# Query transposes of the first two batches by DMA, with weights and loads reordered around them

## The chip, the cores and the metric

The kernel runs on one core of a Trainium2 chip. A core has five engines with instruction queues of their own: PE (TensorE, matmuls), DVE (VectorE), ACT (ScalarE), POOL (GpSimd) and SP (SyncE), which here only issues DMAs. An engine runs its instructions in the order in which they were written; one that waits for data holds up all behind it. Transfers between memory and the core run on 16 DMA engines that POOL's, SP's and ACT's queues share. [...]

The metric is the device time in microseconds of one execution; lower is better.

## The reference

A linear attention with position-dependent features feeds a feed-forward network without a nonlinearity between its last two weights:

```python
def phi(x, c, s):
    r = np.maximum(x, 0.0)
    return np.concatenate([r * c, r * s], axis=-1)   # c, s: cos and sin by position
q_p = phi(q, cos_w, sin_w)
k_p = phi(k, cos_w, sin_w)
kv = np.einsum('bhsf,bhsd->bhfd', k_p, v)
z = np.sum(k_p, axis=2)
num = np.einsum('bhsf,bhfd->bhsd', q_p, kv)
den = np.einsum('bhsf,bhf->bhs', q_p, z)[..., None] + 1e-06
x = (num / den), heads side by side: (4608, 512)
a = x @ w1
b = x @ w2
h = a * b @ w3
return (h @ w_out).astype(np.float32)
```

There are 8 batches of 576 positions, 8 heads of 64, and weights of 512 x 1024 (w1, w2), 1024 x 1024 (w3) and 1024 x 512 (w_out). Inputs and output are float32.

## The kernel before

**Tiling.** A batch's 576 positions are cut into five chunks: four of 128 and one half chunk of 64 (chunk 4). Odd batches begin with the half chunk. The 4608 tokens are nine token tiles of 512. Token tile 0 holds batch 0's chunks 0 to 3; tile 1 holds batch 0's half chunk in its columns 0 to 63, then batch 1's half chunk and its chunks 0, 1 and 2; batch 1's chunk 3 opens tile 2.

**A batch's attention.** POOL issues its loads (`load`), two DMAs for each of k, q and v: the first brings 320 positions to partitions 0 to 63, the second 256 positions to partitions 64 to 127. The DMAs convert to bf16. `prep_k` and `prep_q` make a chunk's features, the cosine half on DVE, the sine half on ACT (L263, L267). `prep_v` copies v beside a column of ones (L287), on DVE for batches 0 and 1, on POOL later. `kv_chunk` multiplies keys by values on PE (L295), and both ACT and DVE copy the sum out. The query features must be transposed to put features on partitions: either on PE with a copy out of PSUM (`q_tr`, L326, L328, L329), or by a DMA transpose that SP issues (L281). `num` (L355) multiplies them by the key-value sum on PE, and DVE divides by the denominator (L371 to L373). `x_tr` transposes the result into the token tile `xT`, again on PE (L407, copy L409) or by a DMA transpose from SP (L403).

Which way a transpose goes depends on the batch. Queries: all five chunks of batch 0 and the first three of batch 1 go through PE, the last two of batch 1 and everything later by DMA (`dma_q`). x: batch 0 and batch 1 but for its chunk 3 go through PE, the rest by DMA.

**The feed-forward network.** For each token tile, `ffn_groups` is a generator: 64 matmuls of x with w1 and w2 (L452), products on ACT and DVE (L457, L458, L505, L509), then 32 matmuls with w34 = w3 @ w_out (L522). w34 is made once, within token tile 0: eight blocks of w3 are transposed on PE (`w3_tr`, L218, copied out by DVE) and multiplied by w_out (`w34_mm`, L230, copied out by ACT at L233). w34_mm of a block has two parts: part 0 uses the first four row groups of w_out, part 1 the last four.

**The order of work.** Nothing is scheduled automatically. `ffn_groups` yields after each group of matmuls, and after yield number s the program writes whatever stands in `slots[s]`. Token tile 0 has slots 0 to 39: w34 is made in slots 16 to 31 (two per block), the last matmuls of the tile stand in slots 32 to 39. Tile 1 begins with slot 40; each later tile has 24 slots. `at(s, ...)` puts a call into a slot; `plan` does so for a batch: kf, qf and vc are the slots of key features, query features and value copies, kv of the key-value matmuls, nu of `num`, xt of `x_tr`. A slot sets only the place in each engine's queue: an instruction runs when its engine reaches it and its data is there. SP's queue holds nothing but two early loads, the transposes and the last stores.

**Loads.** POOL's loads wait on one of eight semaphores in rotation, so a load is issued only once the one eight places before it has landed. `other_loads` issues the rest of w1, w2, then w3 and w_out, with batch 1's keys in between. Loads of batch 2 and later are held back: `plan_loads` puts a one-element copy on ACT (`mark`, L555) into a slot, and POOL waits for that copy (L557) before it issues the load. Stores of the output are held back in the same way until late.

Of the kernel before, what the change touches and what calls it, by code (L numbers as in the profile page):

```python
# [23 lines left out]
def columns_of(b, c):  # L24


    if b % 2 == 0:
        return 128 * c
    return 0 if c == 4 else 64 + 128 * c
# [39 lines left out]
def kernel(  # L69
# [41 lines left out]
    def load(b, which, part=None):  # L111
        for name in which:
            src = {"k": k, "v": v, "q": q}[name]
            if part != 1:
                raw[b, name] = ld.tile([P, H, NCH, D], BF16, name=name + "s",
                                       bufs=2 if name == "q" else 1)
                nc.gpsimd.dma_start(
                    out=raw[b, name][0:64, :, :, :].rearrange("p h j d -> p h (j d)"),
                    in_=src[b, :, 0:320, :].rearrange("h (p j) d -> p h (j d)", j=5))
            if part != 0:  # L120
                nc.gpsimd.dma_start(
                    out=raw[b, name][64:128, :, 0:4, :].rearrange("p h j d -> p h (j d)"),
                    in_=src[b, :, 320:S, :].rearrange("h (p j) d -> p h (j d)", j=4))
# [17 lines left out]
    def load_w3(jp, n):  # L141
        nc.gpsimd.dma_start(out=w3b[:, jp:jp + n, :],
                            in_=moe_w3[ds(jp * P, n * P), :].rearrange("(b p) l -> p b l", p=P))

    def load_wout():
        nc.gpsimd.dma_start(out=woutb[:], in_=moe_w_out.rearrange("(c p) m -> p c m", p=P))

    k0 = raw[0, "k"] = wst.tile([P, H, NCH, D], FP32, name="kf")
    q0 = raw[0, "q"] = ld.tile([P, H, NCH, D], BF16, name="qs", bufs=2)
# [47 lines left out]
    def other_loads(behind):  # L197

        seen = sm.tile([P, 1], BF16, name="seen", bufs=1)
        nc.gpsimd.tensor_copy(out=seen[:], in_=behind)  # L200
        nc.gpsimd.dma_start(out=w2b[:, :, ds(512, 256)], in_=w2v[:, :, ds(512, 256)])  # L201
        load_w12(768, 256)
        for jp in range(2):
            load_w3(jp, 1)
        load_wout()
        for jp in range(2, 4):
            load_w3(jp, 1)
        load(1, "k")
        for jp in range(4, 8, 2):
            load_w3(jp, 2)  # L210


    w3Ts = {}
# [22 lines left out]
    def order_of(b):  # L236

        return [0, 1, 2, 3, 4] if b % 2 == 0 else [4, 0, 1, 2, 3]

    def dma_q(b):  # L240

        return order_of(b)[5 if b < 1 else 3 if b == 1 else 0:]

    feat = {}

# [7 lines left out]
    def att_of(b):  # L253
        if b not in att:
            att[b] = {"qpT": phi.tile([P, H, S], BF16, name="qpT"), "x": {}}
        return att[b]

    def features(b, dst, src, c, cos=True, sin=True, scalar_heads=H):
# [6 lines left out]
        if sin:  # L265
# [3 lines left out]
            if n < H:  # L269
                nc.vector.tensor_scalar(out=dst[:R, c, n:H, D:F], in0=src[:R, n:H, c, :],  # L270
                                        scalar1=0.0, scalar2=sinv[:R, at:at + 1],
                                        op0=ALU.max, op1=ALU.mult)

    def prep_k(b, c):
        features(b, feat_of(b)[0], raw[b, "k"], c)

    def prep_q(b, c):
        features(b, feat_of(b)[1], raw[b, "q"], c)
        if c in dma_q(b):
            R = ROWS[c]  # L280
            nc.sync.dma_start_transpose(out=att_of(b)["qpT"][:, :, ds(columns_of(b, c), R)],  # L281
                                        in_=feat[b][1][:R, c].rearrange("p h f -> p (h f)"))

    def prep_v(b, c):
        R = ROWS[c]
# [35 lines left out]
    def q_tr(b, c, evac=True):  # L321
        R = ROWS[c]
        qp = feat[b][1]
        pst = ps_tr.tile([P, 8, 128], BF16, name="pst")
        for h in range(H):
            nc.tensor.transpose(pst[:, h, :], qp[:, c, h, :], identb[:])  # L326
        dst, src = att_of(b)["qpT"][:, :, ds(columns_of(b, c), R)], pst[:, :, 0:R]
        on_vector = lambda: nc.vector.tensor_copy(out=dst, in_=src)  # L328
        on_scalar = lambda: nc.scalar.copy(out=dst, in_=src)  # L329
        if evac:  # L330
            on_vector()
        return on_vector, on_scalar
# [10 lines left out]
    def num(b, c, chain=True, in_two=False):  # L343
        rows = out_rows(b, c)
        R = ROWS[c]
        at = columns_of(b, c) - rows.start
        qpT, kvs = att[b]["qpT"], att[b]["kvs"]
        if b == 0 and c == 0:
            nt = ps_first.tile([P, 2, 512], FP32, name="pfirst")
        else:  # L350
            pool = more_att[0] if more_att and order_of(b).index(c) % 2 == 0 else ps_att
            nt = None if in_two else pool.tile([P, 2, 512], FP32, name="pnum")
        banks = [ffn_tile(), ffn_tile()] if in_two else [nt[:, g, :] for g in range(2)]
        for h in range(H):
            nc.tensor.matmul(banks[h // 4][:, ds((h % 4) * 65, 65)], lhsT=qpT[:, h, ds(at, 128)],  # L355
                             rhs=kvs[:, h, :], start=True, stop=True)
        if b < 2:
            rows, R = slice(0, P), P
        if in_two:
            parts = [(slice(g, g + 1), t[rows, 0:260].rearrange("p (g h e) -> p g h e", g=1, e=65))  # L360
                     for g, t in enumerate(banks)]
        else:
            parts = [(slice(0, 2), nt[rows, :, 0:260].rearrange("p g (h e) -> p g h e", e=65))]
        xblk = sm.tile([P, 2, 4, D], BF16, name="xblk", bufs=4)
        att[b]["x"][c] = xblk

        def normalize():
            den = sm.tile([P, 2, 4], FP32, name="den")
            for g, n4 in parts:
                G = g.stop - g.start  # L370
                nc.vector.tensor_scalar_add(out=den[rows, g], in0=n4[:, :, :, 64], scalar1=1e-6)  # L371
                nc.vector.reciprocal(out=den[rows, g], in_=den[rows, g])
                nc.vector.tensor_tensor(out=xblk[rows, g], in0=n4[:, :, :, 0:D],  # L373
                                        in1=den[rows, g].unsqueeze(3).to_broadcast([R, G, 4, D]),
                                        op=ALU.mult)

        if chain:
            normalize()
        return normalize
# [11 lines left out]
    def x_tr(b, c, by_vector=False):  # L391
        R, rows = ROWS[c], out_rows(b, c)
        xblk = att[b]["x"].pop(c)
        xf = xblk[:].rearrange("p g h d -> p (g h d)")
        if b % 2 == 0:
            slot = S * b + 128 * c
        else:
            slot = S * b + (0 if c == 4 else 64 + 128 * c)
        t, o = divmod(slot, 512)
        if t not in xT:  # L400
            xT[t] = xtp.tile([P, 4, 512], BF16, name="xT")
        if b >= 2 or (b == 1 and c == 3):
            nc.sync.dma_start_transpose(out=xT[t][:, :, ds(o, R)], in_=xf[rows])  # L403
            return
        pst = ps_tr.tile([P, 8, 128], BF16, name="pst")
        for kc in range(4):
            nc.tensor.transpose(pst[:, kc, :], xf[:, ts(kc, 128)], identb[:])  # L407
        copy = nc.vector.tensor_copy if by_vector else nc.scalar.copy
        copy(out=xT[t][:, :, ds(o, R)], in_=pst[:, 0:4, rows])  # L409
# [139 lines left out]
    def at(s, *calls):  # L549
        slots[s] += calls  # L550
# [8 lines left out]
    def plan(b, kf, vc, kv, qf, nu, loads=None, xt=None):  # L559
        order = order_of(b)  # L560
        for i, c in enumerate(order):
            at(kf[i], lambda c=c: prep_k(b, c))
            at(qf[i], lambda c=c: prep_q(b, c))
            at(vc[i], lambda c=c: prep_v(b, c))
        for i, c in enumerate(order):
            at(kv[i], lambda c=c, i=i: kv_chunk(b, c, i))
        for i, c in enumerate(order):
            at(nu[i], lambda c=c: num(b, c, in_two=b == 1 and c in (0, 2)))
            at(xt[i] if xt else nu[i], lambda c=c: x_tr(b, c, by_vector=(b, c) == (1, 1)))
# [40 lines left out]
    at(1, lambda: x_tr(0, 1, by_vector=True), lambda: q_tr(0, 3, evac=False)[1](), lambda: num(0, 2))  # L610
    at(3, lambda: x_tr(0, 2), lambda: num(0, 3))
    at(5, lambda: x_tr(0, 3))
    at(6, lambda: prep_q(0, 4))
    at(7, lambda: load(1, "qv"), lambda: load(2, "q"))
    at(8, lambda: q_tr(0, 4))
    at(10, lambda: num(0, 4))
    at(11, lambda: feature_buffers(1))
    at(12, lambda: x_tr(0, 4))

    for jp, s in enumerate((13, 15, 17, 19, 22, 24, 26, 28)):  # L620
        at(s, lambda jp=jp: w3_tr(jp))

    plan(1, kf=(22, 23, 24, 25, 26), vc=(31, 31, 32, 32, 32), kv=(33, 33, 33, 34, 34),
         qf=(29, 30, 30, 31, 31), nu=(35, 36, 38, 39, 42), xt=(37, 38, 40, 42, 42))
    for c, s in zip(order_of(1), (31, 32, 34)):
        at(s, lambda c=c: q_tr(1, c))
    at(43, no_more_by_pe)
    plan_loads(2, (27, 28, 33, 35))
    plan(2, kf=(36, 37, 38, 40, 41), vc=(41, 42, 43, 44, 45), kv=(46, 46, 46, 47, 47),
         qf=(40, 41, 42, 43, 44), nu=(48, 50, 52, 54, 57))  # L630
    plan_loads(3, (36, 37, 47, 50, 54, 57))
    plan(3, kf=(54, 57, 59, 61, 63), vc=(64, 65, 66, 67, 68), kv=(71, 72, 72, 73, 73),
         qf=(60, 62, 64, 67, 70), nu=(74, 77, 79, 84, 87))

# [52 lines left out]
```

## Time and profile before

| what | value |
|---|---|
| median of 3 runs | 250.98 us (250.72 to 251.7) |
| profiled execution | 250.3 us |
| its span, first to last instruction | 248.5 us |
| PE busy | 240.4 us, 97% |
| DVE, ACT, POOL busy | 138.6, 130.4, 92.8 us |
| POOL's DMA queue | 27.20 MB |
| SP's DMA queue | 13.38 MB |
| w3 and w_out in use on PE (L218, L230) | 31.1 to about 51 us |
| tile 1 starts on PE | 61.89 us |

The span is what the profile's lines cover; 1.8 us of the execution lie around it. Durations of PE's matmuls overlap each other, since they are pipelined: a group's length in the timeline is from its first start to its last end, and the distance between the starts of two groups is what one costs the queue. A DMA's issue is the short time on POOL or SP; its landing is when its semaphore tells that the data is there.

### The profile page before, as it was taken

Reading aid. Unit: us, or ns where it says so; the run is one execution under the profiler, and the core shown is the slowest. Engines: PE = TensorE matmul, PEld = TensorE weight load, DVE = VectorE, ACT = ScalarE, POOL = GpSimd, SP = SyncE. Lnnn points to the kernel's source line nnn. Section 1 sums busy time; section 2 is a strip of 40 time slices with the busy share of each in tenths; the row PEclk is TensorE's granted clock in tenths of the full one; section 3 lists DMA queues with packets and bytes.
Section 4 is the critical chain, followed back from the end, with each engine's and each line's share of the span. In section 5 each row is a group of like instructions: output and inputs, shape, how many; then the busy total and the mean of one; then the engine's idle time right before and its main releaser. Section 6 shows DMA issues by size and latency. Waiting matters only on the chain.

```text
span 248.5 us, 5036 instructions
## 1 busy us (share of the span) xinstructions
PE 240.4 (97%) x1855; PEld 131.3 (53%) x1884; DVE 138.6 (56%) x337; ACT 130.4 (52%) x267; POOL 92.8 (37%) x195
## 2 busy tenths in 40 slices
PE   8999999999999999999999999999999999999993
PEld 2479555466975445445544555455445554444442
DVE  7775763548967445647665575577465643403320
ACT  2676414677943873476457654854585234334322
POOL 7655332213412261218122612472251009785000
PEclk9999999999999999999999999999999999999999
DMA  7999999999999969999999999999999428997025
GB/s 191 177 193 201 207 204 206 198 174 127 134 189 142 165 103 153 124 148 198 166 135 185 207 172 160 162 188 158 147 201 147 89 42 209 289 301 239 0 46 127
DMA packets 83897, 41.04 MB, mean 165 GB/s; under 512 B 51488, under 2 KB 80416, under 8 KB 83872
## 3 DMA queue, kind: packets, MB, share of 16 engines
q0 software_dynamic: 35456, 27.20, 71.6%
q1 hardware_dynamic: 48256, 13.38, 36.3%
q8 instruction: 15, 0.25, 0.4%
q10 hardware_dynamic: 160, 0.13, 0.2%
q14 instruction: 10, 0.08, 0.1%
HBM read 38.80 MB, written 9.44 MB: 194 GB/s over the span
## 4 chain that ended last, share of the span: by engine, by line
PE 81%; DMA 13%; issue 1%; POOL 1%; DVE 1%; ACT 0%; ACTq 0%; POOLq 0%
PE ffnps L452 44%; PE ffnps L522 24%; DMA w3b<-in_moe_w_dram 6%; PE pnum L355 4%; PE pnum L295 4%; DMA w2b<-in_moe_w_dram 3%; DMA qs<-in_q_dram 3%; PE ffnps L230 3%; PE pst L218 1%; PE pst L326 1%; POOL vs L127 0%; PE pst L407 0%; PE ffnps L538 0%; ACT osb L540 0%; POOL w2b L201 0%
## 5 line engine op out<-in xcount | busy, mean ns | idle before, releaser
L452 PE MATMUL ffnps<-xT,w2b 128*128 128x512 bf16 (+2 forms) x340 | 75.3, 344 | 0.3
L452 PE MATMUL ffnps<-xT,w1b 128*128 128x512 bf16 (+2 forms) x331 | 74.1, 343 | 0.6
L509 DVE TENSOR_TENSOR abT<-asb,ffnps 128x512 bf16<-128x512 bf16 x64 | 43.9, 686 | 51.0 <-PE ffnps L452 49.0
L522 PE MATMUL ffnps<-w34b,abT 128*128 128x512 bf16 x271 | 63.7, 379 | 0.4
L505 ACT CAST asb<-ffnps 128x512 bf16<-128x512 f32 x64 | 37.4, 584 | 50.8 <-PE ffnps L452 46.0
L557 POOL COPY seen<-mark 1x1 bf16<-1x1 bf16 x50 | 9.0, 180 | 97.6 <-ACT mark L555 97.6
L452 PEld LDWEIGHTS <-w2b 128*128 128x128 bf16 x344 | 30.8, 98 | 26.6
L452 PEld LDWEIGHTS <-w1b 128*128 128x128 bf16 x344 | 30.6, 98 | 26.1 <-issue 0.4
L522 PEld LDWEIGHTS <-abT 128*128 128x128 bf16 x280 | 26.0, 98 | 27.9 <-DVE abT L509 0.2
L529 ACT COPY osb<-ffnps 128x512 f32<-128x512 f32 x35 | 20.5, 585 | 35.8 <-PE ffnps L522 35.3
L267 ACT ACTIVATE qp<-qs,sinv 128x512 bf16<-128x512 bf16 (+2 forms) x40 | 28.1, 714 | 1.2 <-DMA qs<-in_q_dram 1.2
L373 DVE TENSOR_TENSOR xblk<-pnum,den 128x512 bf16<-128x512 f32 (+1 forms) x37 | 25.6, 691 | 1.3
L267 ACT ACTIVATE kp<-ks,sinv 128x512 bf16<-128x512 bf16 (+1 forms) x35 | 24.9, 717 | 0.1
L437 POOL DMA_DIRECT2D out_dram<-osb x42 | 22.3, 537 | 3.4 <-issue 3.3
L355 PEld LDWEIGHTS <-qpT 128*128 128x128 bf16 x320 | 15.4, 98 | 8.7 <-DVE qpT L340 0.6
L287 POOL COPY va<-vs 128x512 bf16<-128x512 bf16 (+1 forms) x30 | 17.8, 626 | 5.9 <-DMA vs<-in_v_dram 3.0
L371 DVE TENSOR_SCALAR den<-pnum 128x8 f32<-128x8 f32 (+1 forms) x37 | 6.1, 164 | 22.7 <-PE pnum L355 22.6
L263 DVE TENSOR_SCALAR qp<-qs,cosv 128x512 bf16<-128x512 bf16 (+1 forms) x40 | 17.7, 451 | 0.6 <-DMA qs<-in_q_dram 0.6
L355 PE MATMUL pnum<-kvs,qpT 128*128 128x65 bf16 x296 | 15.8, 194 | 0.1
L230 PE MATMUL ffnps<-woutb,w3T 128*128 128x512 bf16 x62 | 15.2, 380 | 0.1
L295 PEld LDWEIGHTS <-kp 128*128 128x128 bf16 x280 | 11.4, 98 | 4.1
L263 DVE TENSOR_SCALAR kp<-ks,cosv 128x512 bf16<-128x512 bf16 (+1 forms) x35 | 12.7, 371 | 0.0
(86 smaller groups left out, 183.9 us busy)
## 6 DMA issues: line engine op xcount, KB each, us to landing
out_dram<-osb POOLq DMA_DIRECT2D x16, 256.0 KB, 4.5
out_dram<-osb POOLq DMA_DIRECT2D x24, 128.0 KB, 3.9
qs<-in_q_dram POOLq DMA_DIRECT2D x9, 256.0 KB, 8.1
ks<-in_k_dram POOLq DMA_DIRECT2D x7, 320.0 KB, 5.9
qs<-in_q_dram POOLq DMA_DIRECT2D x7, 320.0 KB, 6.4
vs<-in_v_dram POOLq DMA_DIRECT2D x7, 320.0 KB, 6.1
ks<-in_k_dram POOLq DMA_DIRECT2D x7, 256.0 KB, 6.4
vs<-in_v_dram POOLq DMA_DIRECT2D x7, 256.0 KB, 5.6
```

Source lines behind the costliest of these rows:

```text
L230: nc.tensor.matmul(acc[:, :], lhsT=w3T[:, lc, :], rhs=woutb[:, lc, :], start=(lc == 0), stop=(lc == 7))
L263: nc.vector.tensor_scalar(out=dst[:R, c, :, 0:D], in0=src[:R, :, c, :], scalar1=0.0, scalar2=cosv[:R, at:at + 1], op0=ALU.max, op1=ALU.mult)
L267: nc.scalar.activation(out=dst[:R, c, 0:n, D:F], in_=src[:R, 0:n, c, :], func=ACTF.Relu, scale=sinv[:R, at:at + 1], bias=0.0)
L295: nc.tensor.matmul(kvt[:, h // 4, ds((h % 4) * 65, 65)], lhsT=kp[:, c, h, :], rhs=va[:, c, h, 0:D + 1], start=(i == 0 and h % 4 == 0), sto ...
L355: nc.tensor.matmul(banks[h // 4][:, ds((h % 4) * 65, 65)], lhsT=qpT[:, h, ds(at, 128)], rhs=kvs[:, h, :], start=True, stop=True)
L373: nc.vector.tensor_tensor(out=xblk[rows, g], in0=n4[:, :, :, 0:D], in1=den[rows, g].unsqueeze(3).to_broadcast([R, G, 4, D]), op=ALU.mult)
L437: on.dma_start(out=rows[:, :, cols], in_=osb[64 * i:64 * i + rows.shape[0], :, cols])
L452: nc.tensor.matmul(out, lhsT=w[:, kc, ts(jc, 128)], rhs=x[:, kc, tok], start=(kc == 0), stop=(kc == 3))
L505: nc.scalar.copy(out=asb[:], in_=aT[:, :])
L509: nc.vector.tensor_mul(out=abT[:, jc, :], in0=asb[:], in1=bT[:, :])
L522: nc.tensor.matmul(ops[:, :], lhsT=abT[:, jc, ts(ms, 128)], rhs=w34b[:, jc, :], start=(jc == 0), stop=(jc == 7))
L529: nc.scalar.copy(out=osb[:, ms % 2, :], in_=ops[:, :])
```

## The change

- **Half chunk of batch 0.** Its query transpose and its x transpose go from PE to DMA. The features stay at slot 6; the query transpose is written at slot 23 (`transpose_q`, split off from `prep_q`), `num` moves from slot 10 to 29, `x_tr` from 12 to 29.
- **Batch 1's queries.** All five chunks are transposed by DMA; the three `q_tr` calls in slots 31, 32 and 34 go. The query features move from slots 29 to 31 to slots 27 to 29, the key features by up to one slot.
- **Weights.** w_out is loaded in two halves, each behind one of the first two blocks of w3. Batch 1's keys are loaded behind w3 blocks 4 and 5, not before them.
- **Later loads.** Batch 2's keys and values are marked in slots 28, 30, 34 and 37 (27, 28, 33 and 35 before), batch 3's first four loads in 40, 43, 48 and 50 (36, 37, 47 and 50). Batch 2's key features move back a slot.

```diff
-    def load_wout():
-        nc.gpsimd.dma_start(out=woutb[:], in_=moe_w_out.rearrange("(c p) m -> p c m", p=P))
+    def load_wout(half):
+        nc.gpsimd.dma_start(out=woutb[:, ts(half, 4), :],
+                            in_=moe_w_out[ts(half, 512), :].rearrange("(c p) m -> p c m", p=P))
...
         for jp in range(2):
             load_w3(jp, 1)
-        load_wout()
+            load_wout(jp)
         for jp in range(2, 4):
             load_w3(jp, 1)
+        load_w3(4, 2)
         load(1, "k")
-        for jp in range(4, 8, 2):
-            load_w3(jp, 2)
+        load_w3(6, 2)
...
-        return order_of(b)[5 if b < 1 else 3 if b == 1 else 0:]
+        return order_of(b)[5 if b < 1 else 0:]
...
+    def transpose_q(b, c):
+        R = ROWS[c]
+        nc.sync.dma_start_transpose(out=att_of(b)["qpT"][:, :, ds(columns_of(b, c), R)],
+                                    in_=feat[b][1][:R, c].rearrange("p h f -> p (h f)"))
...
         if c in dma_q(b):
-            R = ROWS[c]
-            nc.sync.dma_start_transpose(out=att_of(b)["qpT"][:, :, ds(columns_of(b, c), R)],
-                                        in_=feat[b][1][:R, c].rearrange("p h f -> p (h f)"))
+            transpose_q(b, c)
...
-        if b >= 2 or (b == 1 and c == 3):
+        if b >= 2 or (b, c) in ((0, 4), (1, 3)):
             nc.sync.dma_start_transpose(out=xT[t][:, :, ds(o, R)], in_=xf[rows])
...
-    at(6, lambda: prep_q(0, 4))
+    at(6, lambda: features(0, q0f, q0, 4))
+    at(23, lambda: transpose_q(0, 4))
     at(7, lambda: load(1, "qv"), lambda: load(2, "q"))
-    at(8, lambda: q_tr(0, 4))
-    at(10, lambda: num(0, 4))
+    at(29, lambda: num(0, 4))
     at(11, lambda: feature_buffers(1))
-    at(12, lambda: x_tr(0, 4))
+    at(29, lambda: x_tr(0, 4))
...
-    plan(1, kf=(22, 23, 24, 25, 26), vc=(31, 31, 32, 32, 32), kv=(33, 33, 33, 34, 34),
-         qf=(29, 30, 30, 31, 31), nu=(35, 36, 38, 39, 42), xt=(37, 38, 40, 42, 42))
-    for c, s in zip(order_of(1), (31, 32, 34)):
-        at(s, lambda c=c: q_tr(1, c))
+    plan(1, kf=(23, 24, 25, 25, 26), vc=(31, 31, 32, 32, 32), kv=(33, 33, 33, 34, 34),
+         qf=(27, 28, 28, 29, 29), nu=(35, 36, 38, 39, 42), xt=(37, 38, 40, 42, 42))
     at(43, no_more_by_pe)
-    plan_loads(2, (27, 28, 33, 35))
-    plan(2, kf=(36, 37, 38, 40, 41), vc=(41, 42, 43, 44, 45), kv=(46, 46, 46, 47, 47),
+    plan_loads(2, (28, 30, 34, 37))
+    plan(2, kf=(37, 38, 39, 41, 42), vc=(41, 42, 43, 44, 45), kv=(46, 46, 46, 47, 47),
          qf=(40, 41, 42, 43, 44), nu=(48, 50, 52, 54, 57))
-    plan_loads(3, (36, 37, 47, 50, 54, 57))
+    plan_loads(3, (40, 43, 48, 50, 54, 57))
```

The order of SP's transposes, with c for a chunk, becomes: queries of batch 0 c4; queries of batch 1 c4, c0, c1; x of batch 0 c4; queries of batch 1 c2, c3; then batch 2's.

## The prediction

> **What bounds the kernel now.** I read the page first, then the windows, then the timelines of PE, ACT and SP between 45 and 66 us, then the landing times of single loads.
>
> ```profile
> PE 240.4 (97%) x1855; PEld 131.3 (53%) x1884; DVE 138.6 (56%) x337; ACT 130.4 (52%) x267; POOL 92.8 (37%) x195
> ...
> DMA  7999999999999969999999999999999428997025
> ...
> q0 software_dynamic: 35456, 27.20, 71.6%
> q1 hardware_dynamic: 48256, 13.38, 36.3%
> ...
> PE 81%; DMA 13%; issue 1%; POOL 1%; DVE 1%; ACT 0%; ACTq 0%; POOLq 0%
> ```
>
> PE is busy in 97% of the span, so any PE instruction that goes away is worth its time, unless PE then waits. The DMA row says that the second candidate is close behind: at least nine tenths busy in nearly every slice to 190 us. q0 is POOL's queue (loads, late stores), q1 SP's (the transposes). The last line, from the chain that ended last, has the same two.
>
> ```profile
> 10.00:52.00 42.00, 40.73 (x424) 26.54 (x429) 25.75 (x65) 22.66 (x40) 15.52 (x25) 1.00 1.36 200
> 54.00:62.00 8.00, 7.89 (x102) 5.15 (x101) 5.02 (x16) 4.74 (x14) 3.17 (x8) 1.00 1.05 132
> ```
>
> The windows (last column GB/s): from 10 to 52 us loads alone run at 200 GB/s; once transposes run too, the whole moves 132. Landings in the first stretch follow one another without a gap: batch 1's queries (issued 27.9 and 32.9) at 45.0 and 46.3, its values at 48.0 and 49.3, batch 2's queries at 50.9 and 52.2, batch 2's keys (issued 48.3 and 49.1, landing after 5.6 and 6.4) at 53.9 and 55.5. So this stretch is bound by DMA as well as by PE.
>
> ```profile
> 50.89 0.61 PE L326 MATMUL pst<-identb,qp 128*128 128x128 bf16 x8
> ...
> 52.20 0.61 PE L326 MATMUL pst<-identb,qp 128*128 128x128 bf16 x8
> ...
> 55.64 0.61 PE L326 MATMUL pst<-identb,qp 128*128 128x128 bf16 x8
> ...
> 60.50 0.42 PE L355 MATMUL pnum<-kvs,qpT 128*128 128x65 bf16 x8
> ...
> 61.63 0.42 PE L355 MATMUL ffnps<-kvs,qpT 128*128 128x65 bf16 x8
> 61.89 1.04 PE L452 MATMUL ffnps<-xT,w1b 128*128 128x256 bf16 x8
> ```
>
> PE's timeline: the three query transposes that go, then num of batch 1's chunks 1 and 2 and the start of token tile 1. From 61.89 on PE has no stall to give back: eight tiles of 96 matmuls at 0.216 us, six batches of 40 key-value matmuls at 0.032 and 31 nums at 0.26 are 166 + 7.6 + 8 = 181.6 us, and the last matmul ends near 243.4. So the start of tile 1 carries to the end one for one; I cost the change there.
>
> ```profile
> 52.81 15.20 SPq L281 DMA_TRANSPOSE qpT<-qp  x4
> ```
>
> SP's timeline: its first transpose is issued at 52.8. ACT's timeline:
>
> ```profile
> 57.73 0.72 ACT L267 ACTIVATE kp<-ks,sinv 128x512 bf16<-128x512 bf16 x1
> ...
> 60.84 0.57 ACT L409 COPY xT<-pst 128x512 bf16<-128x512 bf16 x1
> ```
>
> In ACT's order, batch 2's first key features stand ahead of the copy that tile 1 needs.
>
> [...] I counted its packets by queue: between 58.0 and 59.5, where a load of 640-byte packets and a query transpose of 256-byte packets are both under way, they move 304 and 303; between 79.0 and 80.5, with 512-byte packets, 355 and 358. That is 203 and 237 of each per us. Alone, loads of 640 bytes move 263 per us (51 to 52 us) and transposes 1,170 (68.5 to 70). [...] 290 here when alone, but 52 to 61 in company. [...] here eight advance PE by 0.45 us, 56 ns each, and this counts.
>
> **The change part by part.**
>
> PE loses 8 query transposes of batch 0's half chunk, 4 of its x, and 24 of three chunks of batch 1: 36 x 0.056 = 2.0 us. DVE loses four copies (0.42 and 0.69 us) and ACT one (0.38), all beside PE.
>
> The half chunk's query transpose is written at slot 23, but SP has nothing ahead of it and it waits only for features that end at 23.8 us (ACT). So it runs there, among the w3 loads: 512 packets, 0.45 us at their own rate; between 0.4 and 2 us, as around 67 us both queues are nearly silent for 1.5 us in the middle of a transpose. I take 0.45.
>
> The w_out halves cost POOL one more issue (0.7 us, hidden, since up to eight loads are outstanding for some 13 us). Bytes ahead of the second half and of w3 blocks 2 and 3 are the same, so they land at 32.6, 33.9 and 35.4 as before, plus 0.45. PE, 0.93 us earlier by then (8 + 4 transposes and a num of 0.26), wants them at 33.7, 34.6 and 36.7. A few tenths at most; zero. Blocks 4 and 5 go ahead of the keys and land near 38.2 instead of 40.9; they end a wait (PEld on w3b) of which about 0.2 us is PE's. Batch 1's keys land near 41.2, wanted at 41 to 42 behind other ACT work: zero. Blocks 6 and 7 land at 43.8, wanted at 44.3: zero. If the first transpose costs 2 us, these covers are gone and PE loses up to 1.1 of its lead.
>
> The moved num (0.26) stays before tile 1: zero. The q features go from slots 29 to 31 to slots 27 to 29. Behind them on ACT stand two w34 evacuations. Batch 1's second query load lands at 46.7; ACT's run after it is four features at about 0.63, two evacuations at 0.5, a mark: w34 complete near 50.7, needed at 50.8. Zero, but the transposes that used to cover it are gone; each us of later q is a us of stall.
>
> Load marks of batch 2's keys move from slots 27, 28 to 28, 30. As PE is earlier, they fall at about 48.5 and 50.2 us: the same place in a queue that is still backed up. Its values at slots 34 and 37 are issued near 55.5 and 59, before the queue empties. So "later" doesn't thin out the loads here. Batch 3's loads move behind this; no cost.
>
> Now the moved transposes. SP's order is c4, c0, c1 of batch 1, x of the half chunk (behind num and a 1.1 us normalization near 50 us), c2, c3; about 1.25 us of SP each. The first can start to move at about 48.3. In packets: 512, 1024, 1024, 256, 1024, 1024. Loads still to move then: batch 1's values some 600, batch 2's queries, keys and values 1024 each, 3,680 in all. One for one at 220 pairs per us (between 203 and 237):
> - c1 is complete after 2,560 pairs, 11.6 us, at 59.9 (59.1 to 60.9);
> - batch 2's keys after 2,660 load packets, at 60.4, against 55.5;
> - c2 after 3,680 pairs and 160 packets alone, 16.9 us, at 65.2 (64 to 66.5).
>
> What PE wants: num of c1 was at 60.50; less 2.0, plus about 0.1 (the w3 wait gone, the last query transpose no longer covering the kv copies), 58.6. It waits to 60.2 with landing. Then 0.26 for it, 0.86 for four matmuls, and at 61.3 num of c2, which stands in PE's order ahead of tile 1, waits to 65.5. 0.26 later tile 1 starts, near 65.8 against 61.89: +3.9; as some loads may come in gaps, 3.8. Batch 2's keys (60.4, features to 61.1, the xT copy to 61.7) and the half chunk's x (61.5) are late too, but within this wait. c3 is there by 67, wanted at 68. Behind the waiting num stand all PE work, hence DVE's normalizations, and the marks of batch 3's loads: all shift together.
>
> Sum: 248.5 + 3.8 = 252.3 span, 254.1 with the 1.8 us that lie around it. The profiled execution (250.3) is 0.7 under the median of the runs, 250.98; so **254.8**.
>
> **Rivals.** Half a per cent, 1.25 us, is about what a measurement here can tell from no change.
>
> *A, faster.* One mechanism: c2 lands before PE asks for it, at 60.0. It decides together with batch 2's keys landing by 58.5, as their features stand ahead of the xT copy. Then the 2.0 + 0.2 stand: 248.7. For it: the transpose issued at 52.8 landed after 3.6 us, with loads outstanding. Against: then the queue was running dry; and where both ran, 304 x 640 + 303 x 256 bytes in 1.5 us are 181 GB/s, less than the loads' 200 alone, so there is no spare capacity. 0.16.
>
> *B, no difference.* Transposes overtake, at up to 1,170 per us. They still take 4,864 + 512 packets / 1,170 = 4.6 us from the loads: keys at 60.1, features 0.72, xT copy 0.57, tile 1 near 61.6: -0.3 us, 250.7; with half that precedence around 251.5. 0.17.
>
> *C, slower by more.* Silences like that at 67 us come with several of the seven early transposes: 1.5 us in the w3 stage and one or two by 65 us, 256.5 to 258. 0.12.
>
> The forecast: 0.55, its own range 252.4 to 256.3, from the pair rates and up to 1 us of slack either way.
>
> **How the numbers follow.** Faster: A, 0.16. Same: B and the nearest edge, 0.17. Slower: the rest, 0.67. The range leaves out A and the end of C: 250.0 to 257.4.
>
> **What would show it.** Right: no L326 transposes after 20 us on PE; SP's first transpose near 24 us and five from 47; landings of c0 and c1 of 7 us and more, c2 well over 8; a PE wait of some 4 us on the DMA of qpT before tile 1; batch 2's keys landing near 60. Wrong: those landings at 3 to 5 us, or a PE wait on w3, w_out or w34 instead; tile 1 starting before 61.9 means A or B. I would be most wrong if the turns aren't one for one in a deep backlog.

## The result, and the profile after

The changed kernel takes **259.64 us** (median; 258.12 to 261.22) against 250.85 for the kernel before on the same chip: 1.0353 times as long, with an interval of 1.0279 to 1.0427. Two more comparisons of the same pair gave 1.0314 [1.0258, 1.0370] and 1.0288 [1.0208, 1.0369]. It is slower, as forecast, but by some 8.8 us where 3.8 were forecast, and outside the range. Some executions come out slower as a whole (one of e9 below by 4.7 us), and medians and ratios here leave out those more than 1.5% above the fastest of the same kernel.

The profiled execution took 259.72 us with a span of 257.9, 9.4 more than before. Lines of its page, in the order in which those of before were shown (busy time by engine, PE's granted clock and the DMA share in 40 slices, the two queues, the chain by engine and by line). In this kernel the matmuls of x are L456, those with w34 L526, num is L359, the query transpose by DMA L277.

```profile
PE 242.5 (94%) x1848; PEld 130.1 (50%) x1848; DVE 137.2 (53%) x333; ACT 130.1 (50%) x266; POOL 94.2 (37%) x196
...
PEclk9999999985999999999999999999999999999999
...
DMA  7999999999999998999999999999999526898015
...
q0 software_dynamic: 35472, 27.20, 70.0%
q1 hardware_dynamic: 51744, 14.23, 41.4%
...
PE 79%; DMA 16%; DVE 1%; issue 1%; POOL 1%; ACT 1%; ACTq 0%; POOLq 0%
PE ffnps L456 43%; PE ffnps L526 21%; DMA qpT<-qp 10%; PE ffnps L231 5%; DMA qs<-in_q_dram 3%; PE pnum L359 3%; PE pnum L299 3%; DMA ks<-in_k_dram 3%; PE pst L219 1%; PE pst L411 1%; POOL vs L127 0%; PE pst L330 0%; PE ffnps L542 0%; ACT osb L544 0%; DVE xblk L377 0%
```

PE is busy for longer although transposes were taken from it (242.5 against 240.4 us), and the clock row gives a reason: its ninth and tenth slice, 51.6 to 64.5 us, show 8 and 5. (The two sums are not quite comparable: the profile of before lacks 28 of PE's matmul records.) A tenth of the chain is now the DMA of qpT. q1 moved 3,488 packets more, which is just what the five new transposes have: 512 and 256 for the half chunk, 512 and twice 1,024 for batch 1, and 32 small ones with each.

PE's waits between 45 and 75 us (total, number, longest), then PE's timeline there:

```profile
PE ffnps L359 <- DMA qpT<-qp: 3.5, 1, 3.5
PE pnum L359 <- DMA qpT<-qp: 3.3, 1, 3.3
```

```profile
53.48 1.02 PE L526 MATMUL ffnps<-w34b,abT 128*128 128x512 bf16 x4
57.84 0.60 PE L359 MATMUL pnum<-kvs,qpT 128*128 128x65 bf16 x8 [3.33 <-DMA qpT<-qp]
58.24 1.90 PE L526 MATMUL ffnps<-w34b,abT 128*128 128x512 bf16 x4
59.93 0.65 PE L359 MATMUL ffnps<-kvs,qpT 128*128 128x65 bf16 x8
60.39 1.90 PE L526 MATMUL ffnps<-w34b,abT 128*128 128x512 bf16 x4
...
64.37 1.02 PE L526 MATMUL ffnps<-w34b,abT 128*128 128x512 bf16 x4
68.94 0.43 PE L359 MATMUL ffnps<-kvs,qpT 128*128 128x65 bf16 x8 [3.54 <-DMA qpT<-qp]
69.21 1.03 PE L456 MATMUL ffnps<-xT,w1b 128*128 128x256 bf16 x8
```

There are two waits, not one. The first, from 54.5, is that of num of batch 1's half chunk (c4): `num` reads 128 columns of qpT whatever the chunk (`ds(at, 128)` in its matmul), so it needs c0's transpose as well, which landed at 57.70; c4's own had landed at 53.43. The second is num of c2, and tile 1 starts behind it at 69.21, against 61.89 before: 7.3 us later. Between the waits four matmuls that advance PE by 0.86 us take 1.7. The windows (last columns: granted clock, DMA share, GB/s) have the reason:

```profile
10.00:50.00 40.00, 39.27 (x407) 25.31 (x407) 24.05 (x61) 22.58 (x40) 15.16 (x24) 1.00 1.35 199
50.00:70.00 20.00, 13.13 (x119) 7.36 (x118) 6.07 (x23) 6.71 (x15) 4.00 (x8) 0.83 1.51 133
57.00:64.00 7.00, 6.16 (x34) 3.17 (x35) 2.85 (x10) 1.51 (x4) 0.32 (x2) 0.53 1.51 121
```

For nearly all of 57 to 64 us PE ran at half clock: 0.53 granted over this window, 0.5 from 56.72 to 63.55. No half clock follows the second wait (granted 1.0 from 63.55 on). Before 50 us nothing is lost: PE is busy for 98% and loads run at 199 GB/s.

SP's timeline, and the chain that ended last (start, duration, what) from 54 to 136 us:

```profile
46.84 6.24 SPq L277 DMA_TRANSPOSE qpT<-qp  x3
53.14 1.29 SPq L407 DMA_TRANSPOSE xT<-xblk  x1
54.52 9.39 SPq L277 DMA_TRANSPOSE qpT<-qp  x2
```

```profile
54.52 14.37 DMA qpT<-qp
68.89 0.05 issue
68.94 0.43 PE ffnps L359 x8
...
80.66 7.04 DMA ks<-in_k_dram
87.70 0.03 issue
87.72 0.04 DVE kp L264
87.76 0.24 issue
88.00 0.68 DVE abT L513
...
124.69 10.97 DMA qpT<-qp
```

c2's transpose is issued at 54.52 and lands 14.37 us later. Behind the start of tile 1, 0.8 us go at 88.7, where batch 3's key features wait on DVE for a late load and hold up the product that PE needs, and 1.2 us at 135.7, where a num waits for a transpose. The end of PE's work moved from 244.22 to 253.98 us: 7.3 of it at tile 1, the rest behind it.

### The profile page after: what moved, and what is told of

Its sections match the earlier page's. It is cut to its first block, busy times and chain, and to the rows that moved or that the text cites. A ratio compares the mean times of both kernels' runs of the same rounds, so it can differ in the third digit from the quotient of the medians.

```text
span 257.9 us, 5005 instructions
## 1 busy us (share of the span) xinstructions
PE 242.5 (94%) x1848; PEld 130.1 (50%) x1848; DVE 137.2 (53%) x333; ACT 130.1 (50%) x266; POOL 94.2 (37%) x196
## 4 chain that ended last, share of the span: by engine, by line
PE 79%; DMA 16%; DVE 1%; issue 1%; POOL 1%; ACT 1%; ACTq 0%; POOLq 0%
PE ffnps L456 43%; PE ffnps L526 21%; DMA qpT<-qp 10%; PE ffnps L231 5%; DMA qs<-in_q_dram 3%; PE pnum L359 3%; PE pnum L299 3%; DMA ks<-in_k_dram 3%; PE pst L219 1%; PE pst L411 1%; POOL vs L127 0%; PE pst L330 0%; PE ffnps L542 0%; ACT osb L544 0%; DVE xblk L377 0%
## 5 line engine op out<-in xcount | busy, mean ns | idle before, releaser
L456 PE MATMUL ffnps<-xT,w2b 128*128 128x512 bf16 (+2 forms) x344 | 75.5, 344 | 0.0
L456 PE MATMUL ffnps<-xT,w1b 128*128 128x512 bf16 (+2 forms) x344 | 75.5, 344 | 0.0
L526 PE MATMUL ffnps<-w34b,abT 128*128 128x512 bf16 x280 | 67.2, 388 | 0.8 <-DVE abT L513 0.8
L561 POOL COPY seen<-mark 1x1 bf16<-1x1 bf16 x50 | 9.7, 194 | 103.8 <-ACT mark L559 103.8
L456 PEld LDWEIGHTS <-w2b 128*128 128x128 bf16 x344 | 31.0, 98 | 27.3
L456 PEld LDWEIGHTS <-w1b 128*128 128x128 bf16 x344 | 30.7, 98 | 25.9
L526 PEld LDWEIGHTS <-abT 128*128 128x128 bf16 x280 | 26.6, 100 | 30.5 <-issue 1.6
L359 PEld LDWEIGHTS <-qpT 128*128 128x128 bf16 x320 | 15.5, 100 | 18.0 <-DMA qpT<-qp 6.2
L359 PE MATMUL pnum<-kvs,qpT 128*128 128x65 bf16 x296 | 16.0, 195 | 4.6 <-DMA qpT<-qp 4.6
L264 DVE TENSOR_SCALAR qp<-qs,cosv 128x512 bf16<-128x512 bf16 (+1 forms) x40 | 19.2, 487 | 0.7 <-DMA qs<-in_q_dram 0.7
L264 DVE TENSOR_SCALAR kp<-ks,cosv 128x512 bf16<-128x512 bf16 (+1 forms) x35 | 12.1, 353 | 2.5 <-DMA ks<-in_k_dram 2.5
```

Of the source, the lines that this page charges most:

```text
L264: nc.vector.tensor_scalar(out=dst[:R, c, :, 0:D], in0=src[:R, :, c, :], scalar1=0.0, scalar2=cosv[:R, at:at + 1], op0=ALU.max, op1=ALU.mult)
L456: nc.tensor.matmul(out, lhsT=w[:, kc, ts(jc, 128)], rhs=x[:, kc, tok], start=(kc == 0), stop=(kc == 3))
L526: nc.tensor.matmul(ops[:, :], lhsT=abT[:, jc, ts(ms, 128)], rhs=w34b[:, jc, :], start=(jc == 0), stop=(jc == 7))
```

## The experiments

Every ratio is to the kernel before on the same chip, with its 95% interval; "tile 1" is the start of its first matmul (before: 61.89 us).

### One part at a time

The changed kernel with batch 1's first three query chunks back on PE (**e1**):

```diff
-        return order_of(b)[5 if b < 1 else 0:]
+        return order_of(b)[5 if b < 1 else 3 if b == 1 else 0:]
-         qf=(27, 28, 28, 29, 29), ...
+         qf=(29, 30, 30, 31, 31), ...
+    for c, s in zip(order_of(1), (31, 32, 34)):
+        at(s, lambda c=c: q_tr(1, c))
```

> The changed kernel with batch 1's first three query chunks transposed on PE again (features in slots 29 to 31, three PE transposes in 31, 32, 34); half chunk by DMA, w_out halves, key order and later loads stay. Theory (the batch 1 transposes wait in the load backlog, and c2's landing sets tile 1): tile 1 starts at 60.5 to 61.5 and the time is 249.5 to 251. Rival (the later loads make waits of their own after tile 1 has started, 2.1 us in the changed kernel's profile): 252 to 253. Rival (the early half chunk and the weights carry a part): over 253.

251.58 us, 1.0039 [1.0012, 1.0067]; tile 1 at 60.97. The time lies between the ranges of the theory and its rivals: all but 1 us of the loss needs batch 1's transposes, and that 1 us is about what the later loads cost alone (e4 below).

The kernel before with only those transposes by DMA, the same lines the other way round (**e2**):

> The kernel before with one part of the change: all five query chunks of batch 1 by DMA, their features in slots 27 to 29. Theory: PE waits for qpT before tile 1 as in the changed kernel; tile 1 starts at 68 to 70, time 257 to 260. Rival (the wait needs the later loads, or the half chunk's x in SP's queue, beside it): under 255.

254.43 us, 1.0134 [1.0077, 1.0191]. The rival holds: this part alone costs under half of the loss. (Its profile, from an execution 3.4 us above this median, has tile 1 at 67.58.)

The kernel before with only the half chunk by DMA, `features` at slot 6, `transpose_q` at 23, `num` and `x_tr` at 29 (**e3**):

> The kernel before with the half chunk of batch 0 alone moved to DMA (query transpose at 23, num and x at 29). Theory: 12 PE transposes less, 0.7 us, and a transpose that fits between the w3 loads: 250 to 251, tile 1 starts 0.5 to 0.9 earlier. Rival (the early transpose holds up the w3 loads): 251.5 to 253, with PE waiting for w3b.

252.33 us, 1.0057 [1.0032, 1.0082]. The theory missed and the rival is right. PE's waits have the reason. The first line is from e3, in an execution 3.0 us above that median; the second is from e10 below, which has the same half chunk and the same order of weights, in one 1.1 us under its median:

```profile
PE pst L218 <- DMA w3b<-in_moe_w_dram: 1.0, 1, 1.0
```

```profile
PE pst L218 <- DMA w3b<-in_moe_w_dram: 0.9, 1, 0.9
```

With the keys still ahead of w3 blocks 4 and 5, the transpose among the loads makes these late (they landed at 41.45 in e3, at 40.89 before), and the saving on PE turns into a wait.

The kernel before with only the later loads of batches 2 and 3 and the later key features (**e4**):

> The kernel before with only the later slots for the loads of batches 2 and 3 and for batch 2's key features. Theory (later loads leave key features of batch 3 ahead of a product in DVE's queue, waiting for the load): 0.5 to 2 us slower, 251.5 to 253, with a DVE wait on ks near 80 us. Rival (the later waits of the changed kernel come from the transposes still standing in the queue): 250.5 to 251.3, no such wait.

251.59 us, 1.0028 [1.0008, 1.0048]. The time is just in the expected range, but the expected wait of DVE on ks isn't in its profile; where these 0.9 us go stays open.

### Two parts at a time

Batch 1 and half chunk (**e10**, and again **e15**), batch 1 and weights (**e11**), half chunk and weights (**e12**); the weights part is w_out in halves and the keys behind w3 block 5.

> The kernel before with two parts of the change: all of batch 1's queries and batch 0's half chunk by DMA; weights and load slots as before. Alone these took 255.0 and 252.4, together with the weights' new order 260.8. Theory (the half chunk is what turns 255 into 260: its query transpose makes all loads behind it some 1 us later, its x transpose stands ahead of chunk 2's in SP's queue): 258 to 261. Rival (the weights' order does it): 255 to 257.

> The kernel of e10 (before with batch 1's queries and the half chunk by DMA, weights and load slots as before), beside e16 on one chip. Theory (the three parts together are worse than any two): 254 to 256.5, at least 2 us below e16. Rival (the 260.8 of e7 and 259 of the changed kernel against 255.2 of e10 lie in the chips): within 1.5 us of e16.

> The kernel before with all of batch 1's queries by DMA, w_out in halves and the keys behind w3 block 5; half chunk and load slots as before. Theory (the weights' order leaves the number of bytes ahead of batch 1's queries as it was): 254 to 256, as the batch 1 part alone. Rival: 258 to 261.

> The kernel before with the half chunk by DMA, w_out in halves and the keys behind w3 block 5; batch 1's queries and the load slots as before. Theory (12 PE transposes less, and the new order keeps w3 blocks 4 and 5 ahead of PE although the early transpose delays the loads): 249.8 to 250.6, faster than the kernel before by a little. Rival (the half chunk alone, 252.4, loses by more than the wait for w3): 251.3 to 252.5.

e10: 255.24 us, 1.0149 [1.0082, 1.0216]; e15: 254.54, 1.0134 [1.0066, 1.0202]; e11: 254.36, 1.0125 [1.0043, 1.0207]. Neither part adds anything to e2's loss that can be told from noise, so e10's theory fell and e11's held. e12's held too: 250.48 us against 251.06, **0.997 [0.9945, 0.9994]**, with no wait on w3 in its profile. It is the one version with unchanged work that came out below the kernel before, by 0.6 us: under the half per cent named in the prediction, but with an interval below 1.

### The loads of batches 2 and 3

The changed kernel again (**e5**, and **e16** beside e15), with batch 3's loads at the slots of before (**e6**: 36, 37, 47, 50, 54, 57), and with the loads of batches 2 and 3 and batch 2's key features at the slots of before (**e7**):

> The changed kernel once more, so that the next three stand beside it on one chip. 258 to 261; tile 1 starts at 68 to 70.

> The changed kernel on the chip of e15. Theory: 258 to 261. Rival: 254 to 257.

> The changed kernel with batch 3's loads back in their slots of before (36, 37, 47, 50). Theory (what is lost after tile 1 has started, 2.1 us in the profile, comes from batch 3's later loads: key features waiting ahead of a product on DVE): 1 to 2 us faster than the changed kernel, the growth behind tile 1 under 1 us. Rival (it comes from the transposes still standing in the queue): within 0.7 us of the changed kernel, or slower, as two query loads enter the crowded stretch again.

> The changed kernel with the loads of batches 2 and 3 and batch 2's key features back in their slots of before: batch 1's transposes, half chunk, w_out halves and key order remain. Theory (the transposes and the loads' total set the wait before tile 1, the slots hardly matter there): 256.5 to 258.5, tile 1 at 67 to 69. Rival (the later slots make the wait longer than with the batch 1 part alone, 255.0): 254.5 to 256.

e5: 259.01 us, 1.0314 [1.0258, 1.0370]. e16: 258.20, 1.0288 [1.0208, 1.0369], 3.7 us over e15 on the same chip, so the difference between two parts and all of them doesn't lie in the chips. e6: 260.60, 1.0344 [1.0258, 1.0430]. e7: 260.83, 1.0366 [1.0290, 1.0443]. Batch 3's loads aren't the cause of what was lost behind tile 1; that theory fell. e7 is above the ranges of its theory and its rival, and isn't told apart from e5. It is batch 1, half chunk and weights together without the later loads, and the whole loss is there: two of the three cost at most 4.2 us, the three together 7.7 to 10.

Then batch 2's query loads, which stand in the queue ahead of everything else of batch 2, are moved from slot 7 to the slots where batch 1's transposes are already under way (**e8**):

```diff
-    at(7, lambda: load(1, "qv"), lambda: load(2, "q"))
+    at(7, lambda: load(1, "qv"))
+    at(33, lambda: (hold_back(), load(2, "q", 0)))
+    at(35, lambda: (hold_back(), load(2, "q", 1)))
```

> The changed kernel with batch 2's queries not loaded at slot 7 but in slots 33 and 35, so that the backlog behind which batch 1's transposes stand is 0.6 MB (3.2 us at the rate of loads alone) shorter at 47 us. Theory (transposes start only as the backlog of loads runs down): batch 1's chunks 4 and 0 land 2 to 3 us earlier, the first wait of PE, 3.3 us in the changed kernel, is under 1, and the time is 255 to 258. Rival (the number of transposes alone sets it): no landing moves by more than 1 us, 258.5 to 260.

256.58 us, 1.0205 [1.0148, 1.0262]. The theory holds for the first wait: c4 landed at 50.96, not 53.76 as in e5, c0 at 54.49, not 58.28, and the first wait is gone. PE's timeline and a window of e8:

```profile
65.56 0.62 PE L359 MATMUL ffnps<-kvs,qpT 128*128 128x65 bf16 x8 [5.30 <-DMA qpT<-qp]
66.00 1.90 PE L456 MATMUL ffnps<-xT,w1b 128*128 128x256 bf16 x8
```

```profile
64.00:71.00 7.00, 5.44 (x35) 4.16 (x36) 3.24 (x11) 2.63 (x6) 1.63 (x4) 0.52 0.98 141
```

A single wait of 5.3 us for c2 is left, and now the half clock falls into tile 1, which takes 19.3 us to its first w34 matmul, not 17.0.

The loads of batch 2 taken out altogether, from the changed kernel (**e13**) and from the kernel before (**e14**). Both leave out these six DMAs; batch 2 is computed from batch 1's data.

```diff
-    at(7, lambda: load(1, "qv"), lambda: load(2, "q"))
+    at(7, lambda: load(1, "qv"), lambda: raw.update({(2, n): raw[1, n] for n in "kvq"}))
-    plan_loads(2, (28, 30, 34, 37))
```

> The changed kernel without batch 2's loads of k, q and v (six DMAs, 1.77 MB as written): batch 2 computes with batch 1's data, so its rows of the output are those of batch 1. Theory (the transposes are slow and late only because loads stand before and beside them): batch 1's transposes land in 3 to 5 us, PE has no wait for qpT over 0.5 us before tile 1, tile 1 starts at 59.5 to 60.5, time 248 to 249.5, and the PE work saved shows. Rival (five transposes one behind the other are too slow for num by themselves): waits for qpT of over 1 us remain, 251 or more.

> The kernel before without batch 2's loads in the same way (batch 2 computes with batch 1's data), to stand beside e13: both theories 250 to 251, since its PE didn't wait for these loads.

e13: 249.53 us, 0.9954 [0.9934, 0.9974]; e14: 250.48, 0.9984 [0.9961, 1.0008]. Without batch 2's loads the change gains about 1 us. One view for both kernels, that of qpT on SP: the time that SP is held by each of the five query transposes of batch 1 (minimum, median, maximum in ns), and from issue to landing. First the changed kernel (46 to 60 us), then e13 (47 to 58):

```profile
L277 SPq DMA_TRANSPOSE qpT<-qp x5: 1194/3421/5229, 46.8 to 58.7; - x5
...
DMA to landing us min/median/max: 6.6/11.0/14.4
```

```profile
L277 SPq DMA_TRANSPOSE qpT<-qp x5: 1195/1258/2354, 47.4 to 55.2; - x5
...
DMA to landing us min/median/max: 3.3/3.3/3.7
```

The same five transposes land after a median of 3.3 us without batch 2's loads, and of 11.0 beside them; tile 1 starts at 60.09 instead of 69.21. This experiment carries the explanation: without batch 2's loads, ahead of the transposes and beside them, the whole loss is gone. It doesn't separate the loads ahead from those beside; e8 takes only some of those ahead away, and e17 below has the transposes come later.

### When the transposes come, and the clock

The changed kernel with batch 1's query features, and so its transposes, moved back: `qf=(29, 30, 30, 31, 31)` (**e17**, the slots of before) and `qf=(31, 31, 32, 32, 33)` (**e18**). In both, the x transpose of batch 0's half chunk then stands ahead of all five in SP's queue.

> The changed kernel with batch 1's query features, and so its transposes, two slots later (29 to 31, the slots of before, not 27 to 29). In the three profiles of the changed kernel the first of these transposes is issued 6.4 to 6.7 us before batch 2's last query load lands, in e10, e11 and e15 (254.4 to 255.2) 3.9 to 4.1 us before. Theory (the earlier the transposes are issued into the backlog, the longer both sides crawl): issued 3.5 to 5 us before that landing, tile 1 starts at 64 to 66.5, 254 to 256. Rival (the three parts together cost more for another reason): tile 1 at 68.5 to 70, 257.5 to 260.

> The same with the features in slots 31, 31, 32, 32, 33. Theory: issued within 2 us of the backlog's end; the transposes are still beside batch 2's keys and values, so PE waits still, tile 1 at 63.5 to 66, 253.5 to 255.5. Rival as for e17: 257.5 to 260. If both hold in part, the time falls with each step of slots.

e17: 255.97 us, 1.0223 [1.0185, 1.0260]. Its view of qpT on SP, 47 to 60 us:

```profile
L277 SPq DMA_TRANSPOSE qpT<-qp x5: 1222/1261/4366, 50.9 to 59.4; - x5
...
DMA to landing us min/median/max: 4.4/4.9/8.8
```

Issued 4 us later, the transposes land in under half the time by the median, and the last ones earlier in absolute terms: c2 at 62.91 instead of 68.89. Time and tile 1 (66.28) are as the theory said; the lead over the landing, 2.1 us, is shorter than the 3.5 to 5 it had. e18: 256.29, 1.0250 [1.0215, 1.0286], 0.8 over what was expected, with tile 1 at 66.64: moving them further gained nothing. In both runs PE has one long wait left, 4.5 and 4.4 us for c0, whose transpose is now itself late: c4 is issued at 50.88 and 51.35.

The profiles are in nearly the same order as these leads. Where c4 is issued 6.1 to 6.7 us before batch 2's last query load lands (the changed kernel, e5, e6, e7, e16), tile 1 starts at 69.1 to 70.2. Where the lead is 3.9 to 4.1 us (e10, e11, e15), it starts at 64.1 to 66.2, in the profile of e2 at 67.6. With 2.1 (e17) and 1.3 us (e18) it starts at 66.3 and 66.6, but behind the wait for c0. Half chunk and weights together move both ends of the lead: c4 was issued at 47.97 in e7 and at 48.98 in e10, where PE waits 0.9 us each for w3 and for w_out; the last query load landed at 54.09 in e7 and at 51.81 in e11, which has no transpose among the w3 loads. That the transposes suffer from going into a deeper backlog fits the leads and e17; how the depth slows them isn't shown.

What the half clock costs by itself was to be measured by e8 with 20 idle matmuls of 512 columns ahead of num of c2, so that PE doesn't fall idle (**e9**):

> The kernel of e8 (batch 2's queries in slots 33 and 35) with 20 idle matmuls of 512 columns, 4.3 us, on PE right ahead of num of batch 1's chunk 2, where its profile shows a wait of 5.3 us for qpT and then 6.8 us of half TensorE clock. Theory (the wait itself makes the clock fall, and tile 1 runs its first us at half speed): tile 1 starts within 0.7 us of where it did, no half clock follows, tile 1 lasts 2 us less, 254 to 255. Rival (the clock falls for another reason, or the lost us are hidden by later waits): 256 to 257.

255.19 us, 1.0166 [1.0074, 1.0259], not told apart from e8 by these intervals; and its profiled execution was 4.7 us over its median, so that its waits can't be set against e8's. Inconclusive.

## Why the prediction was right or wrong

The direction and the mechanism were right (PE waits for c2 before tile 1, and rivals A and B are out), the size was not: 3.8 us stood for 8.8, and C's 256.5 to 258 was nearer. In the profiled execution tile 1 starts at 69.21, 3.4 us after the predicted 65.8: the packets of c2 were through 0.5 us late, and it landed 3.2 us after that, not 0.3. Another 2.1 us of span were lost behind the start of tile 1, where the prediction had nothing. By its steps:

**The saving on PE, 2.0 us: right up to tile 1.** Without batch 2's loads tile 1 starts at 60.09 (e13), 1.8 us earlier than before and 1.6 earlier than in e14; at the end 1 us of it is left.

**The half chunk's transpose among the loads, 0.45 us; w_out, keys, w3, zero: right together (e12), wrong beside batch 1's transposes.** In e10 the w3 loads behind the transpose landed 0.6 to 0.9 us later than before, and e12 has no w3 wait. That zero rests on the key order: without it the wait is about 1 us (e3, e10). But the prediction added its parts up one by one. Batch 1's transposes with only one of these parts took 254.4 to 255.2 us; that this is where the prediction had put the whole change, 254.8, is luck. All parts together took 3.7 us more (e16 against e15), and for that it had no term.

**Later loads, no cost: nearly right.** e5 and e7 aren't told apart; alone (e4) they cost 0.9 us.

**"One for one at 220 pairs per us", from 48.3: right for the transposes by two errors.** Counted from the trace as for the prediction, no transpose packet moved until 50.8 us, 4 us after the issue, while loads went on at 341 per us; then until 65.68 transposes ran at 258 per us and loads at 112 on average (354 and 86 up to 55 us, 194 and 142 up to 60), not one for one. From 48.3 to 65.68 that is 221 transpose packets per us: the late start and the larger share cancelled out. That packets go one for one had been read off two stretches of 1.5 us of the trace of before (304 and 303 packets, 355 and 358), and didn't hold here. The number that c2's end had been put at, 3,840, was reached at 65.68, and in e5 and e16 at 66.37 and 66.63: 0.5 to 1.4 us past the predicted 65.2.

**"c2 after 3,680 pairs and 160 packets alone, 16.9 us, at 65.2": the step that failed.** It took a transpose to be there when the count of packets is reached, plus 0.3 us. It was there 3.2 us later (68.89), in e5 and e16 2.3 and 2.35 later. c0, which PE wanted first, was late in the same way: its count was reached at 55.93, and it landed at 57.70. The trace shows the parts. Each transpose ends with 32 packets of 4 bytes, which I read as the end marks of the 16 DMA engines that the page counts, two each; that is an estimate, as the trace names no engine for a packet. In e13 those of c2 come within 0.1 us of each other, and the count of 3,840 (55.94), the last mark (55.96) and the landing (56.42) nearly coincide. In the changed kernel 24 of the marks of c2 come between 65.4 and 65.6, two at 66.4, the last six up to 67.70, and the landing another 1.2 us later, when all but 53 packets of c3, the next transpose, had moved too:

```
                      count 3,840   last mark   c2 landed
changed                  65.68        67.70       68.89
changed, e5              66.37        67.97       68.65
changed, e16             66.63        68.52       68.98
two parts, e10           63.51        63.53       64.64
issued later, e17        62.37        62.40       62.91
no loads, e13            55.94        55.96       56.42
```

Read in this way, in the changed kernel a few of the 16 engines had fallen behind, and c2 landed only after the last of them; in e10 and e17, beside loads too, they hadn't: the last mark came 0.02 and 0.03 us after the count. What the traces show without that reading: the last mark comes 1.6 to 2.0 us after the count is reached, in three executions of the changed kernel. In the first of them a DMA has 16 semaphore events, and its landing is the last; those of c2 come from 68.54 to 68.89, all of them after the last mark, and PE starts its num at 68.94. From the last mark to the landing it was 1.2 us in that execution, 0.7 and 0.5 in e5 and e16, and 1.1, 0.5 and 0.5 in e10, e17 and e13. What held back the last marks, and then the landing, isn't shown.

**"PE wants num of c1 at 58.6": wrong place.** I hadn't seen that c4's num reads c0's columns; PE stood from 54.5. By itself this hardly costs anything, as PE would only have waited longer for c2: e8 lacks this wait and has 5.3 us at the next.

**"All shift together", nothing further: wrong by some 2 us.** In the first profile the loss behind the start of tile 1 is the wait for the late keys of batch 3 (0.8) and that for a late transpose (1.2). In e5, e8 and e16 tile 1 itself is 1.5 to 2.3 us longer, and starts at half clock. Nothing in the profile of before showed that clock, so the prediction had no term for it. The traces have stretches of 6.8 us at half clock, granted 0.5 (56.7 to 63.6 in the changed kernel, 63.8 to 70.7 in e8) and of 3.4 us (e5, e16), after waits of 2.9 to 5.3 us. But the wait of 3.54 us before tile 1 in the first profile has no half clock behind it, and e10 has 3.4 us of it though no wait of its PE was over 2.1 us. The granted clock in these traces changes only at steps of 3.41 us (two of them are the 6.83 us from 56.72), and PE's busy share in a step fits better than the length of a wait:

```
                            PE busy   clock in the next step
changed, 53.31 to 56.72       35%     half
changed, 63.55 to 66.96       54%     full
changed, 66.96 to 70.38       42%     full
e10, 56.34 to 59.75           37%     half
e17, 53.40 to 56.82           41%     half
```

The second wait of the changed kernel was cut in two by the end of a step. In the same way, at half clock a step with PE busy for 67% (changed, 56.72 to 60.14) kept it, and one with 79% (e11, 62.99 to 66.41) ended it. Over all 20 profiles of this case, every step at full clock with PE busy for 41% or less is followed by half clock, and every one with 44% or more by full clock; of the three in between one is followed by half. This is read off afterwards; no run was made to test it. In the first profile the half clock lies between the two waits, where PE had to wait for c2 anyway.

**The last 0.7 us, from the profiled execution to the median: gone.** The profile of the changed kernel took 259.72 us, its median is 259.64. Three readings were off without bearing on the sum: between 51 and 52 us loads move 327 packets per us, of which the 263 are those of 640 bytes; from 68.5 to 70 transposes move 1,116 per us, not 1,170, which is 286 GB/s, not 290; and the last matmul of before ends at 244.22, not 243.4.

**The signs named beforehand** came: landings of 7 us and more, c2 well over 8, batch 2's keys at 58.85 and 63.33, PE's wait before tile 1. So did silences, as in rival C: in half-us slots after 60 and from 67 to 68.5 us both queues hardly moved. In the deep backlog the packets didn't go one for one, which was the named danger, but it was the transposes that got more (258 per us), and the loads that lost (112).

**Open:** why an early transpose waits 4 us for its first packet; why both queues together fall to 131 GB/s and at times to a standstill, when loads alone run at 199; what the half clock costs alone; and what of e4's 0.9 us is due to which load.

## What to carry to other kernels

Moving a transpose from PE to DMA was paid here in the latency of that transpose beside the loads that were queued then, not in its packets: a median of 3.3 us without batch 2's loads (e13) became 11.0 in the middle of a backlog (the changed kernel), for a saving of 0.45 us of PE in a full chunk. Estimate when a transfer is there by its last packets and its landing, not by its count: c2's last mark came 2.0 us after the count was reached, and the landing 1.2 us after that. Look at which columns the consumer really reads; and when the sum has PE waiting for 2 us or more, reckon with a stretch of half clock behind it: here such stretches were 3.4 us (e5, e10, e16) or 6.8 us long (the changed kernel, e8). Where it fell into tile 1 it cost some 2 us here (e5, e8, e16). If such a transpose has to go into a backlog, the way out that the runs show is to thin the backlog (e13, e8) or to come later (e17), not to come earlier. And parts that cost nothing one by one may cost something together: add them up only after asking what each does to the time at which the next transfer is issued.

## What the runs showed of the hardware that was not expected

- POOL's loads and SP's DMA transposes shared the engines unevenly in a deep backlog: 4 us from issue to the first packet, then on average 258 against 112 packets per us, at 131 GB/s for both (the changed kernel; with no loads of batch 2 the first packet moves after 1.2 us, e13).
- Transposes that were issued later were done sooner in absolute terms: c2 was issued at 54.52 and landed at 68.89 in the changed kernel, at 58.00 and 62.91 in e17.
- SP was held by the issue of a transpose: mostly for 1.2 to 1.3 us without batch 2's loads (2.4 at most, e13), up to 5.2 us beside the backlog (the changed kernel).
- PE's granted clock fell to 0.5 in the middle of a kernel after waits of as little as 2.1 us (e10), while one of 3.54 us passed without (the changed kernel). In the 20 profiles it did so after every step of 3.41 us at full clock in which PE was busy for 41% or less.
